# Token mixing of the first batch by 128 channels instead of 256, in an attention and MLP-mixer kernel

## The chip, the cores and the metric

The kernel runs on one core of one Trainium2 chip. The metric is the device time of one launch in microseconds (us). The core has five engines that work side by side, each with its own instruction stream: TensorE (PE, matrix products, with its weight loads listed apart as PEld), VectorE (DVE), ScalarE (ACT), GpSimd (POOL) and SyncE (SP). Here POOL and SP mainly start DMA transfers. Engines wait for each other through semaphores.

## What is computed

The inputs are q, k and v of shape (4 batches, 8 heads, 768 positions, 64) and four weight matrices. First comes attention with a window of 128 positions and 4 sink positions that every query sees, and then one token-mixing and one channel-mixing layer on the result:

```
scores = scale * q @ k.T
keep = (key < 4) | (0 <= query - key < 128)
a = softmax(where(keep, scores, -1e9))
x = (a @ v), heads side by side             # (4, 768, 512)
u = x + (relu(x.T @ w_tok1) @ w_tok2).T     # over positions, 768 -> 256 -> 768
out = u + relu(u @ w_ch1) @ w_ch2           # over channels, 512 -> 1536 -> 512
```

## The kernel before

**Units.** Two heads make a pair; there are 16 pairs, four to a batch. A pair's 128 channels are one 128-column strip of x. The window leaves only the diagonal blocks of the score matrix and their neighbours, so that each pair has six key blocks of 128, worked in three groups g of two blocks. For pair p the work units of PE are: `turn` (q and k of the pair transposed, names q and k followed by p), `scores` of a group (s), `score_sinks` for two pairs (x1, x3), and `pv` for half of the queries (o). ScalarE takes the exp of each group from PSUM (line 583); VectorE divides by the sums (lines 651, 654) and so fills x_sb.

**Masks.** The blocks need a triangular mask. There are two ways. `masked` (name m, line 528) lets PE add -32768 by two matmuls with the identity before the scores are accumulated on top; then the exp gives the masked result. Without it, VectorE multiplies the result of the exp by a mask of zeros and ones (line 591), which is one more instruction between exp and pv. In batch 0 the list MASKED_BY_PE (line 69) puts all groups but (3, 0) on PE. Pairs from batch 1 on are all masked by VectorE.

**Token mixing.** `mix_h` (line 752) computes relu(x.T @ w_tok1), `mix_u` (line 780) the second product and u = x + that, and `transpose_u` (line 862, batch 0 only) turns u by PE into uT, which the channel mixing reads. They work on groups of channels: `group` (line 733) makes two groups of 256 channels, two pairs each. A group can begin when both its pairs have their x. In batch 0 each h unit takes one of the two 128-wide tiles of the hidden dimension (6 matmuls of 256 columns), each u unit two of the six position tiles, each t unit four 128x128 transposes. The sum with x is done by VectorE (line 797) or, `by_pe`, by a third matmul with the identity, after which a plain copy by ScalarE or VectorE is enough; three of the six u units of batch 0 have it.

**Channel mixing.** `mix_channels` makes, for each batch, 24 units v1 (two per 128-wide tile of the hidden dimension, for either half of the positions; the evictions are relu by ScalarE or VectorE), then out_part units of three matmuls of 512 columns, whose sums with u VectorE adds (line 1003) and SP stores.

**Order.** A planner, `Plan.run`, emits everything in one order for each engine; it places the evictions on ScalarE or VectorE by estimated costs, and nothing moves at run time. The order of PE is written out: FIRST_BATCH lists the units of attention and token mixing of batch 0; MERGED places the units of the later batches' attention and token mixing ("side"), as number/position, between the channel-mixing units ("main"): 31/55 is side unit 31, behind 55 main units. LOADS is the order of the transfers that POOL starts: v and the number of a pair, q and k (two transfers each), T and A for the token weights, C0 to C3 and D0 to D3 for quarters of the channel weights. Pair 0 to 3's q and k are loaded by SP and cast by ScalarE, VectorE and POOL. q and k of pairs 8 on are turned by DMA transposes on SP's queue, in one stream with the stores. Tiles for q and k rotate over six buffers, v over six. PSUM has two banks for scores ("sc") and four for all else ("mx").

Each pair from batch 1 on also needs `sink_rows`: copies of four rows of v into v_sink by ScalarE or VectorE (line 144 or 142), which wait in that engine's stream for the landing of v; `sink_values` and `values` use them.

Of the kernel before, what the change touches and what calls it, by code (L numbers as in the profile page):

```python
# [10 lines left out]
BF16 = mybir.dt.bfloat16  # L11
# [5 lines left out]
def kernel(  # L17
# [15 lines left out]
    P = 128  # L33
    NT = S // P
    DM = H * D
    DTOK = moe_w_tok1.shape[1]
    DCH = moe_w_ch1.shape[1]
    NC = DM // P
    NF = DCH // P
    NTOK = DTOK // P  # L40
    NHP = H // 2
    HS = S // 2
    D1 = D + 1
# [1 line left out]


    MERGED = (
# [5 lines left out]
    )  # L53
    FIRST_BATCH = (
        "q0 k0 m00 m01 s01 s00 q1 k1 m02 s02 m10 x1 s10 m11 q2 s11 o00 o01 m12 k2 s12 m20 s20 q3 m21 k3 s21 "
        "m22 o11 s22 o10 s30 x3 m31 h01 m32 s31 s32 o20 o21 h00 o30 o31 u02 u00 u04 h10 h11 t00 t02 t04 u10 "
        "u12 u14 t10 t12 t14"
    )
    LOADS = (
        "v1 v2 T0 v3 A0 q4 k4 v4 C0 C1 q5 k5 v5 q6 C2 q7 C3 k6 k7 D0 q8 D1 k8 v6 D2 D3 q9 v7 k9 q10 q11 k10 "  # L60
        "v8 k11 q12 v9 q13 v10 k12 k13 v11 k14 q14 q15 k15 v12 v13 v14 v15"
    )
    NQ = 6
    NPT = 3
# [1 line left out]
    BY_DMA = 8  # L66
    U_LAG = {1: 8000.0, 2: 4000.0, 3: 3500.0}
    U_BY_DMA = [(2, 0), (2, 1), (3, 0), (3, 1)]
    MASKED_BY_PE = [(p, g) for p in range(NHP) for g in range(NT // 2) if (p, g) != (NHP - 1, 0)]

    singles = ctx.enter_context(tc.tile_pool(name="singles", bufs=1))
    qkv_pool = ctx.enter_context(tc.tile_pool(name="qkv", bufs=NQ))
# [12 lines left out]
    def bank(tag, *shape, dtype=FP32, slot=None):  # L85

        n = given[tag].pop(0) if slot is None else slot
        if tag == "sc":
            return sc[n]
        return psum.tile([P, *shape], dtype, name=f"ps_{tag}", tag=f"{tag}{n}", bufs=1)  # L90
# [43 lines left out]
    def mm(*args, **kwargs):  # L134
        in_order(nc.tensor.matmul(*args, skip_group_check=True, **kwargs))  # L135

    def transpose(out, in_):
        in_order(nc.tensor.transpose(out, in_, ident))  # L138
# [7 lines left out]
    def relu(e, out, in_):  # L146
        if e == "ACT":
            in_order(nc.scalar.activation(out, in_, AF.Relu))  # L148
        else:
            in_order(nc.vector.tensor_scalar_max(out=out, in0=in_, scalar1=0.0))  # L150
# [4 lines left out]
    done = {}  # L155
    tiles = {}
# [223 lines left out]
    def unit(ns, fn, deps=(), need=None, then=(), half=False):  # L380

        op = Op({"PE": float(ns)}, fn, deps, then, size=float(ns))
        for f in then:
            if op not in f.deps:
                f.deps.append(op)
        op.need = need or {}
        op.half = half
        return op
# [26 lines left out]
    QH = NT // 2  # L415
# [315 lines left out]


    def group(b, g):
        return g * DM // 2, DM // 2

    def of_group(b, g):
        c0, cn = group(b, g)
        return [done["x", b * NHP + p, half] for p in range(c0 // P, (c0 + cn) // P) for half in range(2)]


    def u_part(b, g, s0, n):
        return tiles["mix", b][1].rearrange("p (g t c) -> p g t c", g=2, t=NT)[:, g, s0:s0 + n]

    def u_rows(b, st):
        return tiles["mix", b][1].rearrange("p (g t c) -> p g t c", g=2, t=NT)[:, :, st]
# [6 lines left out]
    def mix_h(b, g, t0, n):  # L752
        c0, cn = group(b, g)

        def run():
            if ("mix", b) not in tiles:
                tiles["mix", b] = (
                    mix_pool.tile([P, NTOK, DM], BF16, name="h1T"),
                    mix_pool.tile([P, NT * DM], BF16, name="u_sb"),
                    mix_pool.tile([P, NC * S], BF16, name="uT"),  # L760
                )
            ps_h = tiles["ps_h", b, g, t0] = bank("mx", n, cn)
            for tt in range(n):
                for st in range(NT):
                    mm(
                        ps_h[:, tt], w_tok1[:, st, ts(t0 + tt, P)], x_sb[b][:, st, c0:c0 + cn],
                        start=(st == 0), stop=(st == NT - 1),
                    )

        w = n * cn  # L770
        op = Op(
            {"ACT": 190.0 + 0.78 * w, "DVE": 150.0 + 1.05 * w},
            lambda e: relu(e, tiles["mix", b][0][:, t0:t0 + n, c0:c0 + cn], tiles["ps_h", b, g, t0]),
        )
        op.urgent = (1 + g) * (b == 0)
        done.setdefault(("h", b, g), []).append(op)
        return unit(n * NT * cn * 0.422, run, of_group(b, g) + [done["tok1"]], {"mx": [[op]]}, [op])


    def mix_u(b, g, s0, n, by_pe=False):  # L780
        c0, cn = group(b, g)

        def run():
            ps_u = tiles["ps_u", b, g, s0] = bank("mx", n, cn)
            for st in range(n):
                if by_pe:
                    mm(ps_u[:, st], ident, x_sb[b][:, s0 + st, c0:c0 + cn], start=True, stop=False)
                for tt in range(NTOK):
                    mm(
                        ps_u[:, st], w_tok2[:, tt, ts(s0 + st, P)], tiles["mix", b][0][:, tt, c0:c0 + cn],  # L790
                        start=(tt == 0 and not by_pe), stop=(tt == NTOK - 1),
                    )

        def add(e):
            if by_pe:
                return copy(e, u_part(b, g, s0, n), tiles["ps_u", b, g, s0])
            in_order(nc.vector.tensor_tensor(  # L797
                out=u_part(b, g, s0, n), in0=tiles["ps_u", b, g, s0], in1=x_sb[b][:, s0:s0 + n, c0:c0 + cn], op=ALU.add,
            ))

        op = Op({"DVE": 150.0 + 1.05 * n * cn}, add)
        op.urgent = (1 + g) * (b == 0)
        if by_pe:
            op.cost["ACT"] = 190.0 + 0.78 * n * cn
        done["u", b, g, s0] = op
        return unit(n * (NTOK + by_pe) * cn * 0.422, run, done["h", b, g] + [done["tok2"]], {"mx": [[op]]}, [op])
# [52 lines left out]
                done.setdefault(("uT", b, half), []).append(op)  # L859
            plan.pending.append(op)  # L860

    def transpose_u(b, g, s0, n):
        ct0, nct = group(b, g)[0] // P, group(b, g)[1] // P

        def run():
            ps_ut = tiles["ps_ut", b, g, s0] = bank("mx", nct, n * P, dtype=BF16)
            for ct in range(nct):
                for st in range(n):
                    transpose(ps_ut[:, ct, ts(st, P)], u_part(b, g, s0 + st, 1)[:, 0, ts(ct, P)])

        w = nct * n * P
        op = Op(
            {"ACT": 190.0 + 0.78 * w, "DVE": 150.0 + 0.52 * w},
            lambda e: copy(
                e, tiles["mix", b][2].rearrange("c (g t k p) -> c g k t p", g=2, t=NT, p=P)[:, g, :, s0:s0 + n],
                tiles["ps_ut", b, g, s0].rearrange("c k (t p) -> c k t p", p=P),
            ),
        )
        op.urgent = 1 + g
        for half in range(s0 // QH, (s0 + n - 1) // QH + 1):  # L880
            done.setdefault(("uT", b, half), []).append(op)
        return unit(nct * n * 56, run, [done["u", b, g, s0]], {"mx": [[op]]}, [op])

    def first_attention():


        for p in range(NHP):
            prepare(p)
        made = {}
        for p in range(NHP):  # L890
            for n in range(2):
                made["qk"[n] + str(p)] = turn(p, n)
        for p in range(NHP):
            for g in range(NT // 2):
                if (p, g) in MASKED_BY_PE:
                    made[f"m{p}{g}"] = masked(p, g)
                made[f"s{p}{g}"] = burst(scores(p, g))
            if p % 2:
                made[f"x{p}"] = burst(score_sinks(p))
                for n in (p - 1, p):  # L900
                    for half in range(2):
                        made[f"o{n}{half}"] = pv(n, half)
        for g in range(2):
            for t in range(NTOK):
                made[f"h{g}{t}"] = mix_h(0, g, t, 1)
            for st in range(0, NT, 2):
                made[f"u{g}{st}"] = mix_u(0, g, st, 2, (g, st) in [(0, 2), (1, 2), (1, 4)])
            for st in range(0, NT, 2):
                made[f"t{g}{st}"] = transpose_u(0, g, st, 2)
        return [[made[name] for name in FIRST_BATCH.split()]]  # L910

    def attention_and_tokens():

# [184 lines left out]
    for name in LOADS.split():  # L1098
        kind, n = name[0], int(name[1:])
# [67 lines left out]
```

## Time and profile before

| | us |
|---|---|
| median of 3 runs | 201.73 (201.09 to 201.97) |
| the profiled execution | 201.1 |
| its span, first to last instruction | 199.3 |
| PE busy in the span | 190.9 |
| ScalarE busy | 106.1 |
| VectorE busy | 99.7 |
| POOL busy | 67.9 |

A line of the profile names the source line, the engine, the operation, the tiles (out<-in) and the count; then come the busy time, the mean duration of one in ns, and the idle time of the engine just before, with what ended it. In a timeline the two first numbers are the start and the length of a stretch in us, and the note in brackets is the idle time before it. In a table of stretches each engine's busy time stands in the order PE, PEld, DVE, ACT, POOL, followed by the granted clock of PE (1.00 throughout), the DMA share and GB/s.

### The profile page before, as it was taken

What the parts mean: (1) busy time and instruction counts of PE and PEld (TensorE: products, weight loads), DVE (VectorE), ACT (ScalarE), POOL (GpSimd) and SP (SyncE); (2) the same over time, 40 slices, a digit from 0 to 9 for tenths busy, and PEclk for the clock granted to TensorE, in tenths of its full rate; (3) what the DMA queues carried; (4) which work ended last, traced back from release to release, by engine and by line L of the source; (5) the groups of instructions that cost most, each with busy time, mean ns of one, the idle gap of its engine ahead of it and who ended that gap; (6) DMA issues with size and microseconds to landing.
All of it is one profiled execution on the core that took longest, in us unless ns stands there. A gap on an engine that the chain in (4) does not pass through costs nothing.

```text
span 199.3 us, 4761 instructions
## 1 busy us (share of the span) xinstructions
PE 190.9 (96%) x1997; PEld 114.6 (58%) x2015; DVE 99.7 (50%) x215; ACT 106.1 (53%) x185; POOL 67.9 (34%) x86
## 2 busy tenths in 40 slices
PE   6699999999999999999999999999999999999992
PEld 2355885566565665556556755656557746564452
DVE  4777763857867465326367676604235721001222
ACT  4899658988626225868556284776401106771000
POOL 6299869787547723648420000000000000000000
PEclk9999999999999999999999999999999999999999
DMA  6999999999999999999999845100021191000223
GB/s 205 291 258 185 168 183 171 176 183 180 162 150 131 169 150 226 148 208 151 158 155 165 204 103 135 54 2 3 0 99 62 32 230 53 3 0 9 96 109 105
DMA packets 92358, 26.28 MB, mean 132 GB/s; under 512 B 82352, under 2 KB 89392, under 8 KB 92336
## 3 DMA queue, kind: packets, MB, share of 16 engines
q0 software_dynamic: 67232, 11.80, 79.1%
q1 hardware_dynamic: 25104, 14.17, 32.2%
q8 instruction: 16, 0.26, 0.5%
q14 instruction: 6, 0.05, 0.1%
HBM read 26.75 MB, written 6.29 MB: 166 GB/s over the span
## 4 chain that ended last, share of the span: by engine, by line
PE 92%; DMA 3%; ACT 1%; issue 1%; SPq 1%; DVE 0%
PE ps_mx L135 83%; PE ps_sc L135 7%; DMA k_f<-in_k_dram 3%; PE ps_mx L483 1%; PE ps_sc L499 1%; SPq L107 1%; PE ps_mx L138 1%; PE ps_mx L471 0%; ACT pT L583 0%; ACT u_sb L142 0%; DVE k_bf L144 0%; ACT kT L142 0%; DVE o_sb L1041 0%
## 5 line engine op out<-in xcount | busy, mean ns | idle before, releaser
L135 PE MATMUL ps_mx<-w_ch,v1T 128*128 128x512 bf16 (+2 forms) x297 | 65.9, 362 | 0.9 <-issue 0.2
L135 PE MATMUL ps_mx<-uT,w_ch 128*128 128x384 bf16 x384 | 65.8, 326 | 0.0
L148 ACT ACTIVATE v1T<-ps_mx 128x384 bf16<-128x384 f32 x80 | 39.3, 492 | 26.7 <-PE ps_mx L135 14.2
L583 ACT ACTIVATE pT<-ps_sc 128x1024 bf16<-128x1024 f32 (+1 forms) x48 | 44.1, 951 | 12.9 <-PE ps_sc L135 11.6
L135 PEld LDWEIGHTS <-w_ch 128*128 128x128 bf16 x384 | 36.1, 98 | 24.1 <-DVE x_sb L693 0.5
L135 PEld LDWEIGHTS <-v1T 128*128 128x128 bf16 x312 | 28.3, 98 | 26.6 <-issue 0.2
L1003 DVE TENSOR_TENSOR o_sb<-ps_mx,u_sb 128x512 f32<-128x512 f32 x23 | 15.9, 689 | 38.3 <-PE ps_mx L135 32.4
L120 POOL DMA_DIRECT2D q_bf<-in_q_dram x24 | 19.8, 830 | 10.2 <-PE ps_mx L135 2.7
L120 POOL DMA_DIRECT2D k_bf<-in_k_dram x24 | 19.7, 826 | 5.3 <-DMA k_bf<-in_k_dram 3.0
L135 PEld LDWEIGHTS <-w_tok 128*128 128x128 bf16 x192 | 18.1, 98 | 4.8 <-issue 0.5
L128 POOL DMA_DIRECT2D v_aug<-in_v_dram x16 | 16.5, 1037 | 12.4 <-PE ps_mx L135 5.7
L150 DVE TENSOR_SCALAR v1T<-ps_mx 128x384 bf16<-128x384 f32 x16 | 8.8, 553 | 19.8 <-PE ps_mx L135 19.7
L797 DVE TENSOR_TENSOR u_sb<-ps_mx,x_sb 128x512 bf16<-128x512 f32 x21 | 13.8, 687 | 7.6 <-PE ps_mx L135 7.5
L135 PEld LDWEIGHTS <-pT 128*128 128x128 bf16 x352 | 14.5, 98 | 3.8 <-issue 0.3
L135 PE MATMUL ps_mx<-v_aug,pT 128*128 128x65 bf16 x352 | 15.7, 194 | 0.0
L148 ACT ACTIVATE h1T<-ps_mx 128x512 bf16<-128x512 f32 (+1 forms) x9 | 4.5, 503 | 20.8 <-PE ps_mx L135 20.7
L135 PE MATMUL ps_sc<-qT,kT 64*64 64x192 bf16 (+3 forms) x288 | 14.7, 249 | 0.1
L591 DVE TENSOR_TENSOR pT<-pT,mask_main 128x1024 bf16<-128x1024 bf16 (+1 forms) x24 | 14.1, 618 | 0.5 <-ACT pT L583 0.5
L135 PEld LDWEIGHTS <-kT 64*64 64x64 bf16 (+2 forms) x320 | 7.5, 101 | 10.7 <-issue 8.8
L135 PE MATMUL ps_mx<-h1T,w_tok 128*128 128x256 bf16 x96 | 13.2, 273 | 0.0
L135 PE MATMUL ps_mx<-x_sb,w_tok 128*128 128x256 bf16 x96 | 12.0, 273 | 0.1
L693 DVE TENSOR_TENSOR x_sb<-ps_mx,recip 128x384 bf16<-128x384 f32 x22 | 11.8, 551 | 0.2
(64 smaller groups left out, 119.1 us busy)
## 6 DMA issues: line engine op xcount, KB each, us to landing
out_dram<-o_sb SPq DMA_DIRECT2D x23, 256.0 KB, 2.8
v_aug<-in_v_dram POOLq DMA_DIRECT2D x16, 192.0 KB, 9.1
w_ch<-in_moe_w_ch_dram POOLq DMA_DIRECT2D x8, 384.0 KB, 7.7
q_bf<-in_q_dram POOLq DMA_DIRECT2D x24, 96.0 KB, 7.4
k_bf<-in_k_dram POOLq DMA_DIRECT2D x24, 96.0 KB, 8.4
q_f<-in_q_dram SPq DMA_DIRECT2D x4, 384.0 KB, 5.5
k_f<-in_k_dram SPq DMA_DIRECT2D x4, 384.0 KB, 6.0
w_tok<-in_moe_w_tok_dram POOLq DMA_DIRECT2D x2, 384.0 KB, 7.5
```

Source lines behind the costliest of these rows:

```text
L107: in_order(nc.sync.dma_start(out=f, in_=rows_of(pidx, n).rearrange("p h j d -> p h (j d)")))
L120: in_order(nc.gpsimd.dma_start(out=out[:, h], in_=rows[:, h]))
L128: in_order(nc.gpsimd.dma_start(out=v_aug.rearrange("p i t d -> p (i t) d")[:, :, 0:D], in_=v[b].rearrange("h s d -> (h s) d")[2 * hp * S:2 ...
L135: in_order(nc.tensor.matmul(*args, skip_group_check=True, **kwargs))
L138: in_order(nc.tensor.transpose(out, in_, ident))
L148: in_order(nc.scalar.activation(out, in_, AF.Relu))
L150: in_order(nc.vector.tensor_scalar_max(out=out, in0=in_, scalar1=0.0))
L583: in_order(nc.scalar.activation(part(tiles["pT", p][:, :, ds(2 * g, 2)]), of_keys(tiles["ps_s", p, g])[:, :, 0:width(g)], AF.Exp, scale=scale,
L591: in_order(nc.vector.tensor_tensor(out=pt, in0=pt, in1=m, op=ALU.mult))
L693: in_order(nc.vector.tensor_tensor(out=x_sb[b][:, :, ds((2 * hp + i) * D, D)], in0=tiles["ps_o", p, i][:, :, 0:D], in1=tiles["recip", p, i ...
L797: in_order(nc.vector.tensor_tensor(out=u_part(b, g, s0, n), in0=tiles["ps_u", b, g, s0], in1=x_sb[b][:, s0:s0 + n, c0:c0 + cn], op=ALU.add,))
L1003: in_order(nc.vector.tensor_tensor(out=o_sb.rearrange("p (g c) -> p g c", g=2), in1=u_rows(b, st), in0=tiles["ps_out", b, st].rearrange("p ...
```

## The change

- `group`: for batch 0 there are four groups of 128 channels, one pair each. So h needs one pair's x alone; it does both hidden tiles in one unit (12 matmuls of 128 columns). A u unit takes three position tiles (half of the positions), and a t unit the three transposes of that half.
- The add of x by PE is now done for the units named y (y01 and y30, three position tiles of 128 columns each) in place of three units of two tiles of 256 columns.
- A mask unit exists only where FIRST_BATCH names it: m20, m22 and m30 are missing, so VectorE masks groups (2, 0), (2, 2) and (3, 0).
- FIRST_BATCH, MERGED and LOADS are new orders. LOADS is unchanged up to v5.

```diff
-        "0/0 1/2 2/4 3/8 7/11 4/16 6/17 5/17 8/20 10/22 9/22 11/24 12/24 16/26 14/26 17/27 13/30 15/30 18/30 "
-        "19/32 20/35 21/36 22/36 23/39 26/41 25/41 24/41 27/44 31/55 28/63 29/65 30/65 35/66 32/74 34/77 "
-        "43/79 33/79 40/81 41/82 42/83 55/84 36/84 44/84 46/85 37/85 45/85 47/88 39/88 38/88 59/88 49/88 "
-        "48/89 51/90 50/90 52/94 53/95 67/96 54/96 56/112 58/113 57/115 64/119 66/130 68/130 65/131 69/132 "
-        "60/132 70/133 63/133 61/133 62/134 72/134 71/135 73/135"
+        "1/0 0/2 2/5 3/9 7/12 4/17 6/18 5/18 8/21 10/22 9/22 11/24 12/24 15/26 13/27 16/29 14/29 18/29 17/29 "
+        "19/32 20/35 22/36 21/36 23/39 24/41 25/41 26/42 27/44 31/53 28/65 30/67 29/67 32/71 35/76 34/76 "
+        "33/79 40/81 41/82 43/83 42/83 36/83 44/83 46/84 45/87 38/87 55/87 39/87 47/87 37/87 48/88 51/88 "
+        "49/88 50/90 59/92 52/96 54/97 53/99 56/106 58/108 57/109 67/109 60/112 64/113 65/115 66/115 68/119 "
+        "62/122 69/122 70/127 61/128 71/131 73/131 72/131 63/132"
     FIRST_BATCH = (
-        "q0 k0 m00 m01 s01 s00 q1 k1 m02 s02 m10 x1 s10 m11 q2 s11 o00 o01 m12 k2 s12 m20 s20 q3 m21 k3 s21 "
-        "m22 o11 s22 o10 s30 x3 m31 h01 m32 s31 s32 o20 o21 h00 o30 o31 u02 u00 u04 h10 h11 t00 t02 t04 u10 "
-        "u12 u14 t10 t12 t14"
+        "q0 k0 m00 s00 m01 s01 q1 m02 k1 s02 m11 x1 s11 m10 q2 s10 o01 m12 k2 s12 o00 m21 q3 s21 s20 k3 o11 "
+        "s22 x3 o10 m31 s30 s31 o20 h0 m32 o21 s32 h1 o30 o31 y01 u00 h2 u10 u11 t00 h3 u20 t01 t11 y30 t10 "
+        "u21 t20 t30 u31 t31 t21"
     )
     LOADS = (
-        "v1 v2 T0 v3 A0 q4 k4 v4 C0 C1 q5 k5 v5 q6 C2 q7 C3 k6 k7 D0 q8 D1 k8 v6 D2 D3 q9 v7 k9 q10 q11 k10 "
-        "v8 k11 q12 v9 q13 v10 k12 k13 v11 k14 q14 q15 k15 v12 v13 v14 v15"
+        "v1 v2 T0 v3 A0 q4 k4 v4 C0 C1 q5 k5 v5 k6 C2 k7 C3 q6 q7 D0 q8 D1 k8 D2 D3 v6 k9 v7 q9 v8 k10 k11 "
+        "q10 v9 v10 q11 k12 q12 q13 k13 q14 k14 v11 v12 q15 v13 k15 v14 v15"
     )
...
     def group(b, g):
-        return g * DM // 2, DM // 2
+        cn = P if b == 0 else DM // 2
+        return g * cn, cn
...
-    def transpose_u(b, g, s0, n):
+    def transpose_u(b, ct, s0, n):
         def run():
+            ps_ut = tiles["ps_ut", b, ct, s0] = bank("mx", n, P, dtype=BF16)
+            for st in range(n):
+                transpose(ps_ut[:, st], u_part(b, ct, s0 + st, 1)[:, 0])
...
-                if (p, g) in MASKED_BY_PE:
+                if f"m{p}{g}" in names:
                     made[f"m{p}{g}"] = masked(p, g)
...
+        for ct in range(NC):
+            made[f"h{ct}"] = mix_h(0, ct, 0, NTOK)
+            for half in range(2):
+                by_pe = f"y{ct}{half}" in names
+                made["uy"[by_pe] + f"{ct}{half}"] = mix_u(0, ct, half * QH, QH, by_pe)
+                made[f"t{ct}{half}"] = transpose_u(0, ct, half * QH, QH)
```

More of the change, by code (lines that the diff above doesn't have):

```diff
@@ L68 @@
     U_BY_DMA = [(2, 0), (2, 1), (3, 0), (3, 1)]
-    MASKED_BY_PE = [(p, g) for p in range(NHP) for g in range(NT // 2) if (p, g) != (NHP - 1, 0)]
     singles = ctx.enter_context(tc.tile_pool(name="singles", bufs=1))
@@ L741, in u_part @@
     def u_part(b, g, s0, n):
-        return tiles["mix", b][1].rearrange("p (g t c) -> p g t c", g=2, t=NT)[:, g, s0:s0 + n]
+        c0, cn = group(b, g)
+        half, c = divmod(c0, DM // 2)
+        return tiles["mix", b][1].rearrange("p (g t c) -> p g t c", g=2, t=NT)[:, half, s0:s0 + n, c:c + cn]
     def u_rows(b, st):
@@ L860, in transfer_u @@
             plan.pending.append(op)
-    def transpose_u(b, g, s0, n):
-        ct0, nct = group(b, g)[0] // P, group(b, g)[1] // P
+    def transpose_u(b, ct, s0, n):
         def run():
[L866 to L871, printed above, removed]
+            ps_ut = tiles["ps_ut", b, ct, s0] = bank("mx", n, P, dtype=BF16)
+            for st in range(n):
+                transpose(ps_ut[:, st], u_part(b, ct, s0 + st, 1)[:, 0])
         op = Op(
-            {"ACT": 190.0 + 0.78 * w, "DVE": 150.0 + 0.52 * w},
+            {"ACT": 190.0 + 0.78 * n * P, "DVE": 150.0 + 0.52 * n * P},
             lambda e: copy(
-                e, tiles["mix", b][2].rearrange("c (g t k p) -> c g k t p", g=2, t=NT, p=P)[:, g, :, s0:s0 + n],
-                tiles["ps_ut", b, g, s0].rearrange("c k (t p) -> c k t p", p=P),
+                e, tiles["mix", b][2].rearrange("c (g t k p) -> c g k t p", g=2, t=NT, p=P)[:, ct // 2, ct % 2, s0:s0 + n],
+                tiles["ps_ut", b, ct, s0],
             ),
         )
-        op.urgent = 1 + g
+        op.urgent = 1 + ct / 2
         for half in range(s0 // QH, (s0 + n - 1) // QH + 1):
             done.setdefault(("uT", b, half), []).append(op)
-        return unit(nct * n * 56, run, [done["u", b, g, s0]], {"mx": [[op]]}, [op])
+        return unit(n * 56, run, [done["u", b, ct, s0]], {"mx": [[op]]}, [op])
     def first_attention():
@@ L888, in first_attention @@
             prepare(p)
-        made = {}
+        made, names = {}, FIRST_BATCH.split()
         for p in range(NHP):
@@ L902, in first_attention @@
                         made[f"o{n}{half}"] = pv(n, half)
[L903 to L910, printed above, removed]
+        for ct in range(NC):
[4 more added lines that the diff above has]
+                made[f"t{ct}{half}"] = transpose_u(0, ct, half * QH, QH)
+        return [[made[name] for name in names]]
     def attention_and_tokens():
```

## The prediction

> **What bounds the kernel now.** I read the page from the busy shares down, then the waits of TensorE (PE) alone, then the timeline of the first 30 us, where the change lies.
>
> ```profile
> PE 190.9 (96%) x1997; PEld 114.6 (58%) x2015; DVE 99.7 (50%) x215; ACT 106.1 (53%) x185; POOL 67.9 (34%) x86
> ...
> PE   6699999999999999999999999999999999999992
> ...
> PE 92%; DMA 3%; ACT 1%; issue 1%; SPq 1%; DVE 0%
> ```
> ```profile
> PE ps_mx L483 <- DVE k_bf L144: 0.7, 1, 0.7
> PE ps_mx L138 <- ACT u_sb L142: 0.2, 1, 0.2
> PE ps_mx L135 <- issue: 0.2, 1, 0.2
> ```
> ```profile
> 30.00:196.00 166.00, 164.78 (x1625) 97.88 (x1638) 79.83 (x160) 84.73 (x153) 45.70 (x54) 1.00 1.06 118
> ```
> The first fence is the page: PE is in nine tenths of every slice but the first two and the last, and the chain that ended last is 92% PE. The second is all that PE waited for between 9 and 196 us: one cast of the second pair's keys, one copy of u, one gap of issue. The third is the stretch from 30 to 196 us (PE's busy time is the first number after the length): at most 1.2 us of it is idle. So behind the loads of the first 9 us, time is PE work plus 0.9 us or so of waits, and 3.6 us of tail behind PE's last matmul. An edit is worth what it takes from PE's work, less what PE then waits.
>
> **The price of one matmul.**
>
> ```profile
> 6.12 1.04 PE L135 MATMUL ps_sc<-mask_add,ident 128*128 128x512 bf16 x4
> 9.28 0.50 PE L135 MATMUL ps_sc<-mask_add,ident 128*128 128x384 bf16 x2
> 24.55 1.47 PE L135 MATMUL ps_mx<-x_sb,w_tok 128*128 128x256 bf16 x12
> 25.86 0.83 PE L138 MATMUL ps_mx<-ident,u_sb 128*128 128x128 bf16 x12
> 28.28 0.61 PE L138 MATMUL ps_mx<-ident,u_sb 128*128 128x128 bf16 x8
> 29.14 0.40 PE L138 MATMUL ps_mx<-ident,u_sb 128*128 128x128 bf16 x4 [0.24 <-ACT u_sb L142]
> 29.75 1.47 PE L135 MATMUL ps_mx<-uT,w_ch 128*128 128x384 bf16 x8
> ```
> ```profile
> L135 PE MATMUL ps_mx<-x_sb,w_tok 128*128 128x256 bf16 x96 | 12.0, 273 | 0.1
> ...
> L135 PE MATMUL ps_sc<-mask_add,ident 128*128 128x512 bf16 x11 | 3.4, 383 | 0.1
> ...
> L135 PE MATMUL ps_sc<-mask_add,ident 128*128 128x384 bf16 x8 | 2.0, 328 | 0.0
> L138 PE MATMUL ps_mx<-ident,u_sb 128*128 128x128 bf16 x24 | 1.8, 219 | 0.2 <-ACT u_sb L142 0.2
> ```
> Matmuls overlap, so a step is (stretch less one duration) over (count less one): 128 columns (0.83-0.22)/11 = 0.0555 us, 256 columns (1.47-0.27)/11 = 0.109, masks (1.04-0.38)/3 = 0.219 at 512 columns and 0.50-0.33 = 0.17 at 384.
>
> **The change part by part.**
>
> 1. Masks of (pair 2, group 0) and (2, 2) leave PE; (3, 0) had left already. Two matmuls each: -2x0.219 - 2x0.17 = -0.78 us.
> 2. mix_h and mix_u of batch 0 by 128 channels: 48 matmuls of 256 columns become 96 of 128: 96x0.0555 - 48x0.109 = +0.10. The same 24 transposes stay.
> 3. The add of x on PE, three units of two matmuls, is now two units of three, each half as wide: 6x(0.0555-0.109) = -0.32.
>
> PE's work falls by 1.00 us. What of it reaches the end is decided by who feeds PE in the first 29 us.
>
> 4. The front. In FIRST_BATCH m02 now stands before k1, and s00 before m01.
>
> ```profile
> 7.53 1.94 ACT L583 ACTIVATE pT<-ps_sc 128x1024 bf16<-128x1024 f32 x2 [0.43 <-PE ps_sc L135]
> 9.00 0.35 PE L483 MATMUL ps_mx<-ident,k_bf 64*128 64x64 bf16 x12 [0.70 <-DVE k_bf L144]
> 12.21 0.24 PEld L135 LDWEIGHTS <-pT 128*128 128x128 bf16 x6 [0.21 <-DMA v_aug<-in_v_dram]
> 14.75 0.84 POOL L144 CAST k_bf<-k_f 128x768 bf16<-128x768 f32 x1
> 20.50 1.73 ACT L583 ACTIVATE pT<-ps_sc 128x1024 bf16<-128x1024 f32 x2 [0.27 <-PE ps_sc L135]
> ```
> s00 stands behind two mask matmuls in place of four, 2x0.219 = 0.44 less, of which I leave 0.1 to its first half of kT: the first exp starts some 0.35 us sooner than 7.53, and m02 (0.34) falls into the 0.70 us that PE waits for k1. PE is then ahead, but its first pv unit waits for pair 0's values, which release it at 12.21 in the old order, and the same units precede that point in both orders. These gains are spent there; I count 0. If the landing were not the gate, 0.5 would be added.
>
> ```profile
> 23.03 0.27 PE L135 MATMUL ps_mx<-x_sb,ident 128*128 128x256 bf16 x1
> ```
> 5. From 12.2 to the end of o31 (23.03 in the old kernel, where this row, the first of u02, starts). PE has 0.76 less to do: the masks, and 24x0.0555 - 12x0.109 = +0.02 for h0 and h1, which stand here as h00 and h01 did. Walking the new order with the old durations: k3 can't begin before POOL's cast ends (14.75+0.84 = 15.59), which costs 0.4; s30 waits for the exp of s22, 0.3; o31 for the last exp. The old row has that exp ending at 20.50+1.73 = 22.23; ScalarE (ACT) has the same twelve exps, four evictions, two sink exps and first h1T to do, begins 0.35 sooner and loses little: about 21.85. So o31 ends near 22.45, 0.58 sooner, the front's gains being part of what fills these waits.
>
> 6. From there to the first channel product. Old: 23.03 to 29.75, 6.72 us with a wait of 0.42 in it (eight transposes from 28.28 end their steps at 28.72, the next starts 29.14). New, all of 128 columns: y01 9 matmuls, h2 and h3 24, six u units 36, y30 9, six t units 18, that is 96 ahead of the first product, and t31 and t21, 6, behind it: 102x0.0555 = 5.66. With the turn of k4 in place of q4's, 0.44 (29.14+3x0.0555 = 29.31 to 29.75), and 0.1 of waiting for the eviction of t30: 6.2. Gain 0.52.
>
> 7. VectorE (DVE). It gains two mask products, and its adds go from three of 512 columns to six of 384.
>
> ```profile
> L654 DVE TENSOR_TENSOR x_sb<-ps_mx,recip 128x384 bf16<-128x384 f32 x6 | 3.3, 557 | 0.2
> L144 DVE COPY uT<-ps_mx 128x512 bf16<-128x512 bf16 x5 | 2.0, 422 | 1.7 <-PE ps_mx L138 1.5
> ...
> L651 DVE RECIPROCAL recip<-ps_mx 128x6 f32<-128x6 f32 x6 | 1.2, 192 | 1.7 <-PE ps_mx L135 1.6
> L591 DVE TENSOR_TENSOR pT<-pT,mask_first 128x1024 bf16<-128x1024 bf16 x1 | 0.7, 691 | 0.7 <-ACT pT L583 0.7
> L144 DVE COPY kT<-ps_mx 128x384 bf16<-128x384 bf16 x1 | 0.6, 557 | 0.0
> ```
> In the new order it does, from k3's evictions (16.0) to the copy that frees the first product (28.3): 2 kT, 6 reciprocals, 6 norms, 3 masks (all at 0.69, though one is narrower), 5 adds of 384 (priced as the norm, 0.557), 3 uT copies: 1.1+1.2+3.3+2.1+2.8+1.3 = 11.8 of 12.3 us. It is covered with 0.5 to spare, and is what is late next: beyond that PE waits one for one.
>
> 8. MERGED and LOADS, 30 us on. The same matmuls in another order: no work changes, and there is no more than 1.2 us of idle to win; I take 0, between -0.3 and what rival C says.
>
> Sum: 0.58 + 0.52 = 1.1 us, which agrees with 1.0 of work, 0.4 of wait gone and 0.3 of new waits. The profiled execution took 201.1 (span 199.3): 200.0. It was the fastest shown (201.09); on the median 201.73 the same gain gives 200.6.
>
> A rule against part 2. The row: twelve 128-column matmuls, each with its own weight load, in 0.83 us, a step of 0.0555. The Trainium skill, TensorE: Matmul & The Clock Gate, section Back-to-back issue gap, says that in a stream of weight load and matmul the sustained spacing at 128 columns is about 81 ns, and that 56 is only the isolated gap. By it the 102 narrow matmuls would cost 102x0.0255 = 2.6 us more, an estimate from that page, and the sum would come out 1.5 us slower. The trace has the pairs in a stream at 56, so I keep 56.
>
> **The rivals.**
>
> ```profile
> 10.00:15.00 5.00, 4.71 (x90) 2.55 (x90) 3.80 (x9) 4.70 (x7) 5.00 (x7) 1.00 1.73 256
> 15.00:20.00 5.00, 4.87 (x74) 2.88 (x68) 3.55 (x8) 4.85 (x8) 5.00 (x7) 1.00 1.71 186
> ```
> A, the change doesn't reach the end: the saved work turns into waits (VectorE's 0.5 of slack goes, or the exps don't move up). For it: ACT, the fourth engine of these rows, is busy 4.70 and 4.85 of 5 us from 10 to 20. Against it: part 6 needs no exp. It leaves part 3 alone, 0.3: 201.4.
>
> B, slower by its weight loads: each narrow matmul waits out its own load.
>
> ```profile
> L135 PEld LDWEIGHTS <-w_tok 128*128 128x128 bf16 x192 | 18.1, 98 | 4.8 <-issue 0.5 <-DMA w_tok<-in_moe_w_tok_dram 0.3 <-DVE v1T L150 0.2
> ```
> 102x(0.098-0.0555) = +4.3: 204.9. The transposes' 0.0555 speaks against it. The rule of the Trainium skill above is of this kind.
>
> C, slower by one landing: LOADS moves v6 behind the weight quarters D2 and D3.
>
> ```profile
> 42.72 1.03 POOL L128 DMA_DIRECT2D v_aug<-in_v_dram  x1
> 43.73 1.62 POOL L153 DMA_DIRECT2D w_ch<-in_moe_w_ch_dram  x2
> ```
> ```profile
> w_ch<-in_moe_w_ch_dram POOLq DMA_DIRECT2D x2, 384.0 KB, 10.1
> ```
> ```profile
> 54.73 0.33 PE ps_sc L135 x4
> ```
> ```profile
> 51.05 0.52 ACT L142 ACTIVATE v_sink<-v_aug 4x65 bf16<-4x65 bf16 x2
> 59.71 0.54 ACT L142 ACTIVATE v_sink<-v_aug 4x65 bf16<-4x65 bf16 x2 [3.59 <-DMA v_aug<-in_v_dram]
> ```
> ```profile
> DMA to landing us min/median/max: 7.6/11.0/16.3
> ```
> The last row is v_aug's from 30 to 130 us; the row at 54.73 (chain of waits) is the scores of pair 7, behind which pair 6's sinks stand. D2 and D3 are issued by 43.73+1.62 = 45.35 and land 10.1 later, so about 55.4; the three loads together should still end then, now with v6 last. ACT copies its sink rows (0.54; the old copies at 51.05 waited for nothing), done by 56.0, and PE needs them near 56.6: 54.73 - 1.1 + 0.2, and 9x0.219 + 8x0.109 = 2.8 for the 512-column products and two u units that MERGED has put ahead. So 0.6 to spare. Issued at 42.72+1.62 = 44.3, v6 costs the whole gain if it lands 12.8 us later, and decides for slower by 0.5% from 13.8; at 16.3, the longest, the net is +3.5: 205.2. Halfway from 12.8 to 16.3 it is +1.7: 203.4. Against it: the 7.6 of this very load, and that v7 held ACT for 3.59 us while PE went on.
>
> D, another place of the new MERGED stalls, between 60 and 160 us; priced at half of those 3.59 us: 202.4. Against it: the units that hung on late values get them earlier, v8 and v9 being moved ahead of other loads.
>
> **How the numbers follow.** Likeliest 0.60 at 200.6, own range 199.9 to 201.1, four fifths of it below 200.7. A 0.18, C 0.10, B 0.04, D 0.08, half of it beyond 0.5%. Half a per cent (1.0 us) is about what a measurement of this kernel can tell from no change. Faster 0.48; within 0.12+0.18+0.04 = 0.34; slower 0.18. The range 199.8 to 202.8 leaves out B, half of C and a little on both sides, some 0.17.
>
> **What would show it.** Right: nine masked groups on PE, 18 matmuls in place of 22; 128-column steps of 0.056; the first exp near 7.2, the pv start still at 12.2, the last exp of batch 0 ending near 21.85, the first channel product at about 28.5 with six transposes behind it, and from there equal distances. Wrong: a step above 0.06 (B); PE waiting for a VectorE copy or add between 17 and 29 us (A); PE or its loads waiting for v_aug or v_sink near 56.5 (C).

## The result, and the profile after

| | before | after |
|---|---|---|
| median, us | 201.64 (200.90 to 201.97, 6 runs) | 204.56 (203.46 to 205.56, 6 runs) |
| profiled execution, us | 201.09 | 205.56 |
| its span, us | 199.3 | 203.8 |

The ratio is 1.0148, 95% interval 1.0101 to 1.0195: slower by 2.9 us, where 200.6 was forecast. Rival C happened. Medians here are over all executions; ratios and their intervals leave out those more than 1.5% above the fastest of the same kernel. The rows of the changed kernel's page (busy shares, the 40 slices of PE and of its granted clock, the shares of the last chain):

```profile
PE 192.4 (94%) x2041; PEld 116.0 (57%) x2059; DVE 101.6 (50%) x218; ACT 106.6 (52%) x188; POOL 67.6 (33%) x86
...
PE   6887999999949999999999999999999999999993
...
PEclk9999999999996999999999999999999999999999
...
PE 81%; DMA 14%; POOL 1%; DVE 1%; issue 1%; SPq 0%; ACT 0%; POOLq 0%
```

The twelfth slice of PE (56 to 61 us) has fallen from 9 to 4, the clock of the next to 6, and the chain holds 14% DMA in place of 3%. What PE waits for (total, times, longest, us):

```profile
PE ps_mx L134 <- ACT v_sink L141: 3.0, 1, 3.0
PE ps_mx L134 <- DVE ones L161: 1.5, 1, 1.5
PE ps_mx L482 <- POOL k_bf L143: 0.7, 1, 0.7
PE ps_mx L482 <- DVE q_bf L143: 0.5, 1, 0.5
PE ps_mx L482 <- POOL q_bf L143: 0.4, 1, 0.4
```

The first line is the marker that the prediction named for rival C. The chain of waits at that place:

```profile
46.24 14.43 DMA v_aug<-in_v_dram
60.67 0.02 issue
60.69 0.26 ACT v_sink L141
```

v6 is issued at 46.24 and lands 14.43 us later, at 60.67, 5.9 us behind D3, which landed at 54.74. ScalarE, whose order has the copy of v6's sink rows there, stands until then. PE's timeline (the number in brackets is its idle time):

```profile
57.60 0.39 PE L134 MATMUL ps_sc<-qT,kT 64*128 64x256 bf16 x4
61.00 0.66 PE L134 MATMUL ps_mx<-v_sink,pT_sink 64*128 64x65 bf16 x8 [3.01 <-ACT v_sink L141]
```

And by stretches (length, then busy time of PE, PEld, DVE, ACT, POOL, then PE's granted clock, DMA share, GB/s):

```profile
57.00:61.00 4.00, 1.00 (x8) 0.31 (x6) 0.75 (x2) 0.28 (x2) 0.03 (x1) 1.00 3.16 109
61.00:64.50 3.50, 3.18 (x36) 2.41 (x37) 1.43 (x5) 1.77 (x4) 3.50 (x5) 0.52 2.45 158
64.50:68.00 3.50, 3.45 (x76) 1.92 (x76) 2.67 (x6) 1.46 (x2) 3.50 (x5) 0.99 1.70 162
```

PE is idle for 3 us, and then, working again, is granted half its clock for 3.4 us. By these rows the place costs 3.0 + 3.4/2 = 4.7 us.

The first batch, where the gain was expected, looks like this:

```profile
23.68 0.22 PE L134 MATMUL ps_mx<-x_sb,ident 128*128 128x128 bf16 x1
...
24.51 0.83 PE L134 MATMUL ps_mx<-x_sb,w_tok 128*128 128x128 bf16 x12
...
29.54 0.82 PE L134 MATMUL ps_mx<-uT,w_ch 128*128 128x384 bf16 x4
30.20 0.50 PE L137 MATMUL ps_mx<-ident,u_sb 128*128 128x128 bf16 x6
```

The token stage starts at 23.68 (old: 23.03) and the first channel product at 29.54 (old: 29.75), with six transposes left behind it. A row of twelve 128-column matmuls takes 0.83, a step of 0.0555.

### The profile page after: what moved, and what is told of

It is laid out like the page before. It is cut to its first block, busy times and chain, and to the rows that moved or that the text cites. A ratio compares the mean times of both kernels' runs of the same rounds, so it can differ in the third digit from the quotient of the medians.

```text
span 203.8 us, 4864 instructions
## 1 busy us (share of the span) xinstructions
PE 192.4 (94%) x2041; PEld 116.0 (57%) x2059; DVE 101.6 (50%) x218; ACT 106.6 (52%) x188; POOL 67.6 (33%) x86
## 4 chain that ended last, share of the span: by engine, by line
PE 81%; DMA 14%; POOL 1%; DVE 1%; issue 1%; SPq 0%; ACT 0%; POOLq 0%
PE ps_mx L134 75%; DMA v_aug<-in_v_dram 7%; PE ps_sc L134 4%; DMA w_tok<-in_moe_w_tok_dram 4%; DMA v_sink_f<-in_v_dram 3%; POOL v_aug L127 1%; PE ps_mx L137 1%; SPq L213 0%; PE ps_sc L498 0%; PE ps_mx L470 0%; POOL v_sink L143 0%; PE ps_mx L482 0%; ACT v_sink L141 0%; DVE v_sink_f L209 0%; DVE mask_add L178 0%
## 5 line engine op out<-in xcount | busy, mean ns | idle before, releaser
L134 PE MATMUL ps_mx<-uT,w_ch 128*128 128x384 bf16 x384 | 66.8, 326 | 0.0
L147 ACT ACTIVATE v1T<-ps_mx 128x384 bf16<-128x384 f32 x82 | 40.2, 491 | 32.1 <-PE ps_mx L134 18.3
L134 PEld LDWEIGHTS <-w_tok 128*128 128x128 bf16 x240 | 19.5, 98 | 5.4 <-issue 0.6
L799 DVE TENSOR_TENSOR u_sb<-ps_mx,x_sb 128x512 bf16<-128x512 f32 (+1 forms) x24 | 15.4, 654 | 11.0 <-PE ps_mx L134 11.0
L149 DVE TENSOR_SCALAR v1T<-ps_mx 128x384 bf16<-128x384 f32 x14 | 7.7, 554 | 21.5 <-PE ps_mx L134 21.4
L134 PEld LDWEIGHTS <-pT 128*128 128x128 bf16 x352 | 15.1, 100 | 3.8 <-issue 1.1
L134 PE MATMUL ps_mx<-v_aug,pT 128*128 128x65 bf16 x352 | 16.4, 197 | 0.2 <-DMA v_aug<-in_v_dram 0.2
L590 DVE TENSOR_TENSOR pT<-pT,mask_main 128x768 bf16<-128x768 bf16 (+1 forms) x25 | 14.7, 615 | 1.3 <-ACT pT L582 1.3
L134 PE MATMUL ps_mx<-h1T,w_tok 128*128 128x256 bf16 (+1 forms) x120 | 14.6, 256 | 0.0
L134 PE MATMUL ps_mx<-x_sb,w_tok 128*128 128x256 bf16 (+1 forms) x120 | 12.2, 251 | 0.2 <-DMA w_tok<-in_moe_w_tok_dram 0.2
## 6 DMA issues: line engine op xcount, KB each, us to landing
v_aug<-in_v_dram POOLq DMA_DIRECT2D x16, 192.0 KB, 10.5
```

The costliest lines, as they stand in the source:

```text
L590: in_order(nc.vector.tensor_tensor(out=pt, in0=pt, in1=m, op=ALU.mult))
L799: in_order(nc.vector.tensor_tensor(out=u_part(b, g, s0, n), in0=tiles["ps_u", b, g, s0], in1=x_sb[b][:, s0:s0 + n, c0:c0 + cn], op=ALU.add,))
```

## The experiments

Theory L: the late landing of v6 is the whole loss. Against it stand F (the narrower first batch costs time) and M (the new MERGED does). Ratios are to the kernel before, run beside them. Of each edit only the part of a line that changes is shown, with `...` for the rest.

**1. v6 put back, in the changed kernel (new_v6_early)**

```diff
-... D1 k8 D2 D3 v6 k9 v7 ...
+... D1 k8 v6 D2 D3 k9 v7 ...
```

> The changed kernel with v6 put back ahead of D2 and D3 in LOADS, nothing else. Theory L (one late landing is the whole loss): v6 lands near 51 in place of 60.67, PE's 3.0 us wait for v_sink and the 3.4 us of halved clock behind it go, 3.0 + 1.7 = 4.7 us: 204.56 - 4.7 = 199.9 by the median, 205.56 - 4.7 = 200.9 by the profiled execution, so 199.7 to 201.2. Rival F (the narrower first batch costs time of its own) or rival M (the new MERGED order does): 202 or more, since the wait was then only part of the loss. Rival S (the landing is late for another reason than its place, the pair's transposes that SP issues at 50): v6 still lands after 57 and the time stays within 1 us of 204.6.

200.52 us, ratio 0.9942 (0.9920 to 0.9963). v6 is issued at 43.69 and lands at 51.27. By stretches:

```profile
50.00:60.00 10.00, 9.89 (x103) 6.09 (x104) 7.28 (x17) 4.96 (x9) 4.79 (x7) 1.00 1.83 144
60.00:80.00 20.00, 19.84 (x258) 11.54 (x259) 12.25 (x24) 8.66 (x16) 10.94 (x14) 1.00 1.90 170
```

The wait and the halved clock are gone, and 4.0 us with them, where the rows had 4.7. F and M as causes of the loss fall; so does S as it was put (what the late place brings v6 beside is asked in experiment 4).

**2. v6 moved back, in the old kernel (old_v6_late)**

```diff
-... D1 k8 v6 D2 D3 q9 v7 ...
+... D1 k8 D2 D3 v6 q9 v7 ...
```

> The kernel before with v6 moved behind D2 and D3 in LOADS, nothing else. Theory L: v6, issued near 44.4 in place of 42.7, lands after 57 in place of 50.3, PE waits for v_sink where pair 6's sinks stand (near 55 in the old order) for 2 us or more and its granted clock drops behind that: 204 to 206.5 in place of 201.6. If v6 lands by 55.5 (right behind D3's 55.4) there is no wait, the move alone is not the cause, and the time is 201.3 to 202. Rivals F and M (first batch, MERGED): 201.3 to 202, since neither is in it.

207.16 us, ratio 1.0280 (1.0247 to 1.0312): the move of one name costs 5.5 us. v6 is issued at 44.59 and lands 13.7 us later, at 58.31. PE's timeline, then the stretches:

```profile
54.47 0.39 PE L135 MATMUL ps_sc<-qT,kT 64*128 64x256 bf16 x4
58.64 0.66 PE L135 MATMUL ps_mx<-v_sink,pT_sink 64*128 64x65 bf16 x8 [3.77 <-ACT v_sink L142]
```
```profile
55.00:57.00 2.00, 0.00 (x0) 0.00 (x0) 0.00 (x0) 0.00 (x0) 0.11 (x1) 0.99 1.63 133
57.00:59.00 2.00, 0.30 (x6) 0.18 (x7) 0.00 (x0) 0.62 (x3) 0.00 (x0) 0.50 2.40 154
59.00:63.80 4.80, 4.80 (x30) 2.52 (x30) 1.83 (x4) 1.42 (x3) 4.53 (x6) 0.50 2.08 149
63.80:67.00 3.20, 3.15 (x29) 2.00 (x28) 2.35 (x6) 0.00 (x0) 3.20 (x5) 1.00 2.43 154
```

The wait is 3.8 us, and half clock from 58.64 to 63.8 costs another 2.6, which makes 6.4 by the rows against the 5.5 measured; 207.16 lies above the expected range. In the changed kernel PE came to pair 6's sinks 3.1 us later (57.99 against 54.86) and v6 landed 2.4 us later, so that its wait is the shorter one.

**3. The old LOADS in the changed kernel (new_old_loads)**

> The changed kernel with the whole LOADS order of the kernel before (first batch and MERGED new). Theory L: no wait for v_sink near 57, 199.7 to 201.2. If other moves of LOADS (q6 and k6, v8 ahead of k10) are worth something by themselves, this stands above the run with v6 alone put back, by 0.3 or more. Rivals F or M: 202 or more.

200.23 us, ratio 0.9934 (0.9911 to 0.9958), within the interval of experiment 1: the other moves in LOADS are worth nothing that can be told. Of the versions that are told apart from the kernel before (experiments 1, 3, 7 and 10) this has the lowest median.

**4. Why v6 lands late: pair 8 turned by PE (new_pair8_on_pe).** Pair 8 is the first whose q and k SP turns by DMA, and its two transposes are issued at 47.14 and 50.25 in the changed kernel.

```diff
-    BY_DMA = 8
+    BY_DMA = 9
```

> The changed kernel, LOADS and all, but pair 8's q and k are turned by PE in place of the two DMA transposes that SP issues at 47 and 50 us (first pair turned by DMA is 9, not 8); v6 stays behind D2 and D3. PE gets 24 more small transposes, about 0.7 us. Theory T (v6's 256-byte packets lose the DMA engines to pair 8's transposes): v6 lands within 2 us of D3, by 57, the wait at pair 6's sinks is under 0.5 us, no halved clock, 200.5 + 0.7 = 201.2, between 200.7 and 202.2. Theory Q (the place behind D2 and D3 alone makes it late): v6 lands after 59, a wait of 1.5 us or more, 203.5 or more.

201.95 us, ratio 1.0007 (0.9979 to 1.0034). D3 lands at 54.41 and v6 1.5 us behind it, at 55.92; PE waits for no sink row. The load's row in the DMA issues (KB, us from issue to landing) of this run, then in the changed kernel:

```profile
v_aug<-in_v_dram POOLq DMA_DIRECT2D x1, 192.0 KB, 9.3
```
```profile
v_aug<-in_v_dram POOLq DMA_DIRECT2D x1, 192.0 KB, 14.4
```

Theory T holds: same place in the queue, and 5 us less. In the changed kernel's trace POOL's queue moves 1208 to 1226 packets in each us from 60 to 64, when SP's moves at most 16, and 384 to 775 from 55 to 58, beside 130 to 400 of SP's; from 52 to 54 it moves 521 against SP's 526, one for one. The Trainium skill, DMA: Bandwidth & Descriptors, section Rules for kernel authors, says of DMAs from several engines that they "all run on the same 16 DMA engines and interleave"; these counts agree. The sharing is not all of the delay. Twelve of the sixteen engines have done their share of v6 by 57.73, the last four only at 59.56 to 60.67, and between them the trace has a standstill:

```profile
58.25:59.50 1.25, 0.00 (x0) 0.00 (x0) 0.00 (x0) 0.00 (x0) 0.00 (x0) 1.00 1.46 14
```

The last number, 14 GB/s, is 154 from 60 to 62.5. In these 1.25 us the two queues move 83 and 29 packets. The trace of this experiment has no such stretch between 52 and 60, so it goes with the transposes; why is not shown.

The time is 1.4 above experiment 1, where 0.7 was expected for the transposes on PE; the profile also has the latest first add of all, 24.11, and what else it lost was not asked.

**5. Why it costs more than the wait (new_wait_filled)**

```diff
-            (by_quarters if quarters else by_halves)(tiles["ps_s", p, g])
+            for _ in range(14 if (p, g) == (7, 0) else 1):
+                (by_quarters if quarters else by_halves)(tiles["ps_s", p, g])
```

> The changed kernel with the wait filled: the four score matmuls of pair 7, first mask group, are issued 14 times in place of once (the same result written again), 13 x 0.23 = 3.0 us more PE work just ahead of pair 6's sinks; nothing is left out. Theory G (the halved clock comes from PE's idle 3 us): v6 still lands near 60.5, PE waits for v_sink by 0.5 us or less, the granted clock stays at 1.00 between 50 and 80, and the time is 204.56 less half of 3.4 us: 202.9, between 202.2 and 203.6. If the clock falls all the same, or the filler comes on top of the wait: 204.5 or more.

203.34 us, ratio 1.0088 (1.0056 to 1.0120). ScalarE's copy still stands behind the landing, at 59.89 here, and PE's clock stays:

```profile
59.91 0.54 ACT L141 ACTIVATE v_sink<-v_aug 4x65 bf16<-4x65 bf16 x2 [6.50 <-DMA v_aug<-in_v_dram]
```
```profile
50.00:60.00 10.00, 9.95 (x115) 6.71 (x115) 5.54 (x11) 3.35 (x7) 3.16 (x4) 1.00 2.27 132
60.00:80.00 20.00, 19.69 (x281) 11.70 (x282) 12.67 (x25) 8.62 (x15) 12.20 (x15) 1.00 1.92 173
```

With 3 us of useless work more, the kernel is 1.2 us faster than the changed one. All four of its executions have a mean granted clock of 1.000; of the changed kernel's six, five have 0.992, and the one with 1.000 took 203.46. So the halved clock follows PE's idleness, in most executions. Its price is loose: 1.7 by the rows, 1.2 by these medians, whose intervals touch (1.0101 to 1.0195 for the changed kernel) and of which part can be v6's landing, 0.8 earlier here; and 1.0 is what experiment 1's 4.0 leaves beside a wait of 3.0.

**6. The first batch alone (first_batch_alone):** the changed kernel with the old MERGED and LOADS.

> The kernel before with the new first batch alone (MERGED and LOADS as before). Prediction's steps 1 to 7: 1.1 us less than before, 200.5 by the median. By the profile of the changed kernel, whose first channel product came only 0.2 sooner than before with six transposes (0.33) left behind it, the gain is about nothing: 201.4 to 202. The two are told apart by the place of the first channel product, 28.5 or 29.5, and by whether the first loads (v1 landing at 15.7 before, 16.2 in the changed kernel's profile) come late here too. Rival F: over 202.5.

The median is 202.83, the single times run from 200.67 to 207.48, and the ratio without the three longest is 1.0013 (0.9975 to 1.0051). The profiled execution is the longest; it is shown because it holds a likely cause. What PE and what ScalarE waited for:

```profile
PE ps_sc L134 <- ACT pT L582: 4.0, 1, 4.0
```
```profile
ACT v_sink L141 <- DMA v_aug<-in_v_dram: 6.0, 1, 6.0
```

It is v6's story again: v13, issued at 97.80 beside the transposes of the last pairs, lands after 14.2 us, at 111.97, ScalarE stands before its sink rows, PE waits 4.0 us for the exp behind them, and the clock is 0.50 from 114.0 to 117.4.

**7. The same with v12 and v13 earlier (first_batch_v13_early)**

```diff
-... k14 q14 q15 k15 v12 v13 v14 v15
+... k14 v12 q14 v13 q15 k15 v14 v15
```

> The run with the first batch alone, with v12 put ahead of q14 and v13 ahead of q15 in the old LOADS, nothing else. Theory T again: v13, which landed 14.2 us after its issue beside the transposes of pairs 14 and 15, lands several us sooner, no wait for its sink rows near 110, spread under 1.5 us, median 200.7 to 201.3 in place of 202.83. If the wide spread had another cause, it stays: median 202 or more and runs above 203.

200.90 us, ratio 0.9956 (0.9933 to 0.9978), all twelve times between 199.71 and 201.60. The long executions are gone with v13's late place, so that the last stage has the same trap.

**8. The same edit in the old kernel (old_v13_early)**

> The kernel before with v12 put ahead of q14 and v13 ahead of q15 in LOADS, nothing else. It prices the first batch without the wait for v13: the first batch with these two loads early was 200.90. If the first batch itself is worth the 1.1 us that the prediction gave it, this comes out at 201.5 to 202.0, the spread narrower than the 200.7 to 205.0 that the kernel before had. If the first batch is worth nothing and the gain of the last run was all v13, this is at 200.7 to 201.1.

201.36 us, ratio 0.9977 (0.9952 to 1.0001): between the two expectations. Of the gain of experiment 7, half is v13's place by these ratios, and 0.9977 - 0.9956 = 0.2%, about 0.4 us, comes with the first batch. The intervals overlap and this one reaches 1, so both sizes are loose.

**9. MERGED alone (merged_alone):** the old kernel with the new MERGED.

> The kernel before with the new MERGED order alone (first batch and LOADS as before). The changed kernel with the old LOADS gave 200.23, the first batch alone 201.9 over its undisturbed executions, with 200.7 the best and a 4.0 us wait for v13 in the profiled one. Theory: MERGED's part is that it needs v13's rows later, so that wait can't occur, 200.5 to 201.3 and a narrow spread. If the gain of 1.4 us is all of the first batch, this stays at 201.4 to 202.

201.99 us, ratio 1.0013 (0.9988 to 1.0038), times from 200.92 to 203.47. A miss: no gain and no narrow spread. ScalarE waits for no sink row after 85 us in its profile, but that is the fastest execution, so that it can't say what slows the others; this stays open.

**10. What ate step 5: POOL's cast (new_v6_early_k3_first).** In the profile of experiment 7, PE waits for POOL's casts of pair 3's queries and keys, as in the changed kernel's:

```profile
PE ps_mx L482 <- POOL k_bf L143: 0.7, 1, 0.7
PE ps_mx L482 <- POOL q_bf L143: 0.6, 1, 0.6
```

The edit, on experiment 1, puts the cast of pair 3's keys ahead of the load A0 on POOL (the second number is the time at which the planner thinks the keys have landed):

```diff
-... (13500.0, 14700.0) ...
+... (13500.0, 13600.0) ...
```

> The changed kernel with v6 ahead of D2 and D3, and POOL's cast of pair 3's keys put ahead of the load A0; PE's order and all other queues' stay (VectorE changes two neighbours). With v6 early alone it was 200.52. Theory P (what ate the 0.58 us of the prediction's step 5 is POOL: in four profiles of the new first batch PE waits 0.7 us for the cast of pair 3's keys and up to 0.6 for its queries): the 0.7 us wait goes, the first PE add of x comes at 22.4 to 22.9 in executions whose clock is full from the start, against 23.05 to 24.1 now, and the time is 199.7 to 200.2. Rival E (the exps or pair 0's values set the leg, and the cast's wait only takes the place of theirs): the first add stays later than 23.0 and the time is 200.4 to 200.8. Rival A0 (the load moved back by 0.85 us lands too late for the second token product): a wait for w_tok near 23.5 and 201 or more.

200.91 us, ratio 0.9963 (0.9933 to 0.9994): no gain over experiment 1, and a miss of theory P's 199.7 to 200.2. Ten of the twelve executions took 200.36 to 202.43, two 223 and 1090 us, which nothing here explains. The wait for the cast is gone and the first add comes at 22.87, as theory P has it, but the next wait takes it:

```profile
29.36 0.34 PE L134 MATMUL ps_mx<-uT,w_ch 128*128 128x384 bf16 x1 [0.56 <-DMA w_ch<-in_moe_w_ch_dram]
```

**11. C0 and C1 earlier too (new_k3_and_c0_first)**

```diff
-... A0 q4 k4 v4 C0 C1 q5 ...
+... A0 q4 k4 C0 C1 v4 q5 ...
```

> The run with v6 early and k3's cast early, with the channel weights C0 and C1 also put ahead of v4 in LOADS; PE's order is unchanged. Theory W (with the cast out of the way the first channel product waits for C0, 0.6 us in the last profile, where C0 landed at 29.31): C0 lands by 28.2, that wait goes, the first channel product comes at 28.9 or earlier, and the time is 199.9 to 200.4 in place of 200.91. If the front's savings are taken by yet another wait, the first product stays at 29.2 or later and the time at 200.5 to 201.0; if v4, moved back by 1.5 us, comes late for pair 4, a wait for v_sink or v_aug shows between 33 and 40.

201.36 us, ratio 0.9973 (0.9938 to 1.0008), times from 199.53 to 203.55: inconclusive. The profiled execution (199.85) shows what theory W says: C0 lands at 26.38, and

```profile
22.29 0.22 PE L134 MATMUL ps_mx<-x_sb,ident 128*128 128x128 bf16 x1
...
28.15 0.82 PE L134 MATMUL ps_mx<-uT,w_ch 128*128 128x384 bf16 x4
```

All executions but one were longer than this, for a reason that no profile caught.

## Why the prediction was wrong, point by point

**Steps 1 to 3, PE's work: right.** PE has 2041 matmuls against 1997, the 48 more of step 2 less the four masks of step 1, and the step at 128 columns is the predicted 0.0555. Rival B falls with it: of the Trainium skill's two spacings (TensorE: Matmul & The Clock Gate, section Back-to-back issue gap) the stream here runs at the 56 ns one.

**Step 4, nothing gained ahead of pair 0's values: right, and a little worse.** The first exp starts at 7.13 (forecast 7.2). The first pv unit starts with a sink product at 12.11 (12.2), but its values landed at 12.46, 0.4 later than in the old kernel, and hold PE there:

```profile
12.50 0.28 PE L134 MATMUL ps_mx<-v_aug,pT 128*128 128x65 bf16 x4 [0.16 <-DMA v_aug<-in_v_dram]
```

**Step 5, 0.58 us up to the end of o31: failed.** The first add was forecast at 22.45, the end of the last exp at 21.85; the changed kernel has 23.68 and 23.07, the eight other profiles with the new first batch 22.29 to 24.11. Only experiment 11, where the cast of pair 3's keys stands ahead of A0 and POOL starts early (8.27), reaches the forecast. The step priced the wait for that cast at 0.4, from the old profile's end of it, 15.59. Here POOL's work on the first loads starts 0.6 to 1.4 us later in six of nine profiles with the new first batch (cast of the first sink rows at 9.38 to 9.89, against 8.51 to 8.76 in the four with the old one), k3's cast ends later by as much, and PE waits 0.7 for it and 0.4 for q3's. It was said that the saved work could turn into waits here (rival A), but it was put down to VectorE and the exps. What POOL waits for there is the landing of the first sink rows, in the old kernel and in the changed one:

```profile
8.51 0.91 POOL L144 CAST v_sink<-v_sink_f 128x520 bf16<-128x520 f32 x1 [3.81 <-DMA v_sink_f<-in_v_dram]
```
```profile
9.62 0.61 POOL L143 CAST v_sink<-v_sink_f 128x520 bf16<-128x520 f32 x1 [4.92 <-DMA v_sink_f<-in_v_dram]
```

SP starts these four small loads between 2.8 and 4.4 us in every profile; why they land later in some was not found.

**Step 6, 0.52 from there to the first channel product: right.** 29.54 - 23.68 = 5.86 with six transposes (0.33) to come, 6.19 in all against the forecast 6.2.

**Step 7, VectorE: right.** PE waits for no copy or add of VectorE's between 17 and 29 us.

**Step 8, MERGED and LOADS at nothing: the step that failed, and nearly all of the loss.** Rival C had the place, the load and the waiter, but three of its terms were off. Its landing, which is what failed: "the three loads together should still end then" took the queue to be served in order at an even rate, with v6 at 55.4; D3 was even early, but v6's packets shared the engines with pair 8's transposes, 60.67. Its start: v6 was issued at 46.24, not 44.3, POOL running 1.4 late from 23 us on and waiting 0.59 more before v6, while PE needed it at 57.99, not 56.6, so 11.75 us were left between the two, not 12.3. And its price had no clock: 14.43 us to land makes the wait 3.0, and half clock adds 1.0 to 1.7 (experiment 5). The 16.3 among the old landings was in view and taken for the end of a range; it was v9's, issued at 65.91 while SP issued five transposes between 61.67 and 78.16, and the move put v6 beside two. With the transposes in the sum, C would have been the main case and not a chance of 0.10.

Without that place the forecast total is met, 200.52 in experiment 1 against 200.6, but in good part by luck. The spans of that profile and the old one are 198.5 and 199.3. PE reaches the same point of its work, the first channel product and the six transposes behind it, 0.3 sooner (29.11 + 0.33 against 29.75), where steps 5 and 6 had 1.1; over the seven profiles with the new first batch and without the edits of experiments 10 and 11 it is 29.25 to 30.30, over the four with the old one 29.55 to 30.59. The work from there to PE's last matmul is the same within 0.1. The remaining 0.57 lies in the tail behind that matmul, 3.08 against 3.65, which the prediction took as fixed. SP's last three stores, old and then experiment 1:

```profile
194.82 2.13 SPq L1046 DMA_DIRECT2D out_dram<-o_sb  x3
```
```profile
194.60 1.54 SPq L1043 DMA_DIRECT2D out_dram<-o_sb  x3
```

The first of the three takes 0.85 to 1.22 to issue in the four profiles with the old first batch and 0.33 in the nine with the new one, whose tails are 3.06 to 3.26 against 3.35 to 3.72. Why is not shown, and no step of the prediction has it; so the 0.4 of experiment 8 need not be the mixing by 128 channels at all. That the new orders avoid v13's late landing can be part of the gain too, but experiment 9, with the new MERGED alone, gained nothing.

## What to carry to other kernels

When a load changes places in a queue, ask what else will be on the DMA engines while it is in flight: a load of 128-byte packets that landed 9.3 us after its issue took 14.4 from the same place of the queue beside two DMA transposes. A load whose waiter stands in order on an engine that everything passes (here ScalarE) is worth issuing early, as the move of one name cost 5.5 us in the old kernel. And a stop of PE by 3 us is to be priced with the halved clock that can follow, here 1.0 to 1.7 us. Last, where a total agrees, compare the parts: here most of the gain in span lay in a tail that the prediction took as fixed.

## What the runs showed of the hardware beyond what was expected

- PE's clock fell to half at idle stretches of 3.0, 3.8 and 4.0 us (the changed kernel, experiments 2 and 6), for 3.4, 6.8 and 3.4 us. It fell 3.1, 2.1 and 4.3 us after PE's last matmul: in the second during the idleness, in the others only when PE was at work again. The Trainium skill, TensorE: Matmul & The Clock Gate, section What's actually happening, has a free-running window of 3413 ns; the lengths, about one, two and one of these, agree. The same section of the Trainium skill names an idle window of about 3.4 us or more as what throttles the clock; here 3.0 us of idleness was enough in the first case and 2.1 in the second.
- The clock's first rise moves by itself: the full clock was granted from 4.1 to 6.5 us on in eleven profiles, and only from 10.5 and 10.0 in those of experiments 1 and 3, whose spans were nevertheless 198.5.
- DMA packets of two queues went one for one (521 and 526 from 52 to 54 in the changed kernel), and while the last packets of the two transposes went, the DMA engines all but stood for 1.25 us (14 GB/s).
